# The last product of a retention and two-layer MoE kernel as seven half products

## The chip, the cores and the metric

The kernel runs on one core of one Trainium2 chip. The metric is the device time of one execution in microseconds, as the median of several runs. The profile shows one execution: TensorE (PE; its weight loads are PEld), VectorE (DVE), ScalarE (ACT), GpSimd (POOL), the DMA queues issued from SP, ACT and POOL, and the TensorE clock that was granted.

## The reference

```python
# q, k, v: (8, 8, 576, 64)
gamma = 1 - 2.0 ** (-5 - arange(8))                 # one per head
Dmat  = where(i >= j, gamma ** (i - j), 0)
x     = ((q @ k.T / 8) * Dmat) @ v                  # -> 4608 tokens x 512
a, b  = x @ w1, x @ w2                              # 512 x 1024 each
x2    = ((a * b) @ w3) @ w_out                      # 1024 x 1024, 1024 x 512
h     = x2 @ w_in2                                  # 512 x 2048
g     = h * clip(h + 3, 0, 6) / 6
out   = g @ w_out2                                  # 2048 x 512
```

The weights arrive as 64-bit floats. The kernel decodes each piece to 32 bits with two ScalarE and two VectorE operations (`weights`, L132).

## The kernel before, in words

Every large product is made from operands that are split in a high and a low part (a ScalarE cast writes the high part, a VectorE subtraction the low part): `mm3` (L123) issues three matmuls, high x high, high x low and low x high, into one bank of PSUM. Each matmul comes with its own weight load of 128x128.

The order of the work is written out by hand. `at(s, f)` (L113) puts a function into slot `s`; each `mm3`, and each matmul of the prologue, first calls `tick()` (L116), which runs the functions of the present slot. A slot fixes where an instruction stands in its engine's program, not when it runs: engines run their programs in order, and waits on data are added by the framework.

Four stages follow each other:

1. **Prologue** (L450 to L476). 32 matmuls of 256 columns on zeros warm TensorE up, and then `w3 @ w_out` is computed into `Wh`, `Wl` (eight tiles `Wps`, four banks, so the fifth tile waits until the first is read out by `w_hi` and `w_lo`). Beside it the first pieces of w1 and w2 are loaded and decoded (`order12`, L414), and the first attention tiles run as "excursions" (`ex`, L433): scores of tile t+1, then the products of tile t; a mask on VectorE (`p_mask`) follows the scores one slot later.
2. **moe1** (`ffn1`, L493): nine blocks of 512 tokens, 96 `mm3` each, with the excursions between them. It ends each half block with x2's operand sums for the next stage, stored to DRAM (`xod`), through the staging tiles `stg` and `stg_hi`. The blocks also hold jobs that prepare weights and store them to DRAM: `job_set` (L604) makes the seven sums of a pair of w_in2 pieces (`wid`), `job_q` (L626) decodes one of sixteen pieces of w_out2 (`wqd`). `E0` is the start of the last block.
3. **moe2's first product** (`run_set`, L733): six blocks of 768 tokens, eight sets each, already as seven half products per set (Strassen's scheme, Winograd's form), with 384 columns per matmul. `gate` (L705) makes g from each result and GpSimd's queue stores it to DRAM (`gd`).
4. **moe2's last product** (L829 to L864): nine blocks of 512 tokens. For each of 16 pieces of the 2048 inner columns g is loaded (`load_g`, two pieces per DMA), split (`g_hi`, `g_lo`) into one of two buffers, and used as the stationary operand for four groups of 128 tokens: `mm3` with 512 columns of w_out2 (all loaded before, `load_wq`). After 16 pieces ScalarE copies four banks out with the factor 1/6, and SP's queue stores them (`store`, L834).

```python
for t in range(BLK2 // 128):
    ...
    ts = slice(t * 128, t * 128 + 128)
    mm3(acc[t], gh[:, ts], gl[:, ts], w[:, m % 4, 0], w[:, m % 4, 1], m == 0, m == M2 - 1)
```

## Time and profile before

| | |
|---|---|
| median of 3 runs | 1514.9 us (1514.26 to 1515.38) |
| the profiled execution's own time | 1514.79 us |
| its span, first to last instruction | 1513.0 us |
| TensorE busy | 1497.9 us (99%) |
| VectorE, ScalarE, GpSimd busy | 775.7, 534.7, 254.5 us |
| granted TensorE clock, mean | 0.999 |
| moe2's last product, first to last matmul start | 1116.4 to 1508.9 us |

The page gives shares over the whole span; a stage has to be read from windows or from its own tiles. Busy time is the time in which at least one instruction of the engine runs; matmuls are pipelined and their records overlap, so the spacing of starts, not a record's length, says how fast they go. The profiled execution's time is 1.8 us longer than its span.

### The profile page before, as it was taken

To read this page: it belongs to the slowest core of one execution; us is meant where nothing else is said; L and a number is where in the kernel's file an instruction comes from. 1 tells how busy PE (TensorE), PEld (TensorE's weight loads), DVE (VectorE), ACT (ScalarE), POOL (GpSimd) and SP (SyncE) were. 2 spreads that over 40 slices of the span, in tenths; PEclk is the share of its full clock that TensorE was granted. 3 is DMA by queue.
4 is the path that set the end of the run, shared out by engine and by line. 5 is a ranking of instruction groups with operands and counts; after the bars stand their busy time and mean duration, and the time that the engine had idled before them with its cause. 6 is when DMAs were issued, how large, how long until landed. Compare 5 with 4: busy or idle time off the path is not lost. (4 is left out here: it accounts for less than half of the span.)

```text
span 1513.0 us, 23506 instructions
## 1 busy us (share of the span) xinstructions
PE 1497.9 (99%) x9248; PEld 1273.2 (84%) x9248; DVE 775.7 (51%) x1449; ACT 534.7 (35%) x883; POOL 254.5 (17%) x460
## 2 busy tenths in 40 slices
PE   8899999999999999999999999999999999999999
PEld 4478888888888888888899999999988888888887
DVE  6886565565655565653256666666652222222222
ACT  6473333333333342332233333333332222222222
POOL 3313212222222212200012323223310000000000
PEclk9999999999999999999999999999999999999999
DMA  9853647465656654524689464464872223333320
GB/s 326 255 181 98 215 147 217 152 209 162 202 167 182 202 167 161 182 91 145 256 324 344 170 260 171 190 251 154 329 262 104 91 91 133 139 139 140 139 84 28
DMA packets 121295, 274.58 MB, mean 181 GB/s; under 512 B 12784, under 2 KB 55792, under 8 KB 120160
## 3 DMA queue, kind: packets, MB, share of 16 engines
q1 hardware_dynamic: 48288, 144.72, 27.2%
q0 software_dynamic: 25856, 75.93, 15.6%
q10 hardware_dynamic: 47040, 52.43, 10.1%
q8 instruction: 72, 1.18, 0.3%
q14 instruction: 39, 0.32, 0.1%
HBM read 169.75 MB, written 103.28 MB: 180 GB/s over the span
## 5 line engine op out<-in xcount | busy, mean ns | idle before, releaser
L130 DVE TENSOR_TENSOR ghl<-gr,ghl 128x512 fp32r<-128x512 f32 x144 | 99.7, 693 | 287.7 <-ACT ghl L805 285.6
L125 PE MATMUL pb<-xop,wset 128*128 128x384 f32 x672 | 225.8, 336 | 2.6 <-DVE stghi L700 1.5
L127 PE MATMUL pb<-xop,wset 128*128 128x384 f32 x672 | 225.8, 336 | 0.0
L126 PE MATMUL pb<-xop,wset 128*128 128x384 f32 x672 | 225.5, 336 | 0.0
L127 PE MATMUL po<-wq,ghl 128*128 128x512 f32 x576 | 224.3, 389 | 0.0
L125 PE MATMUL po<-wq,ghl 128*128 128x512 f32 x576 | 224.2, 389 | 0.0
L126 PE MATMUL po<-wq,ghl 128*128 128x512 f32 x576 | 224.1, 389 | 0.0
L805 ACT CAST ghl<-gr 128x512 fp32r<-128x512 f32 x144 | 89.5, 622 | 275.8 <-PE po L127 275.7
L719 POOL DMA_DIRECT2D gd<-g x192 | 104.4, 544 | 361.4 <-DVE g L714 222.1
L186 POOL DMA_DIRECT2D qk<-in_qk_dram x144 | 84.6, 594 | 433.3 <-PE z L233 362.7
L710 ACT ACTIVATE stghi<-g,three 128x384 f32<-128x384 f32 x141 | 87.1, 617 | 128.8 <-DVE g L700 128.6
L125 PEld LDWEIGHTS pb<-xop,wset 128*128 128x128 f32 x672 | 126.2, 188 | 4.1 <-DVE stghi L700 1.9
L127 PEld LDWEIGHTS po<-wq,ghl 128*128 128x128 f32 x576 | 108.1, 188 | 23.4 <-DVE ghl L130 0.9
L125 PEld LDWEIGHTS po<-wq,ghl 128*128 128x128 f32 x576 | 108.1, 188 | 22.8 <-ACT ghl L805 0.5
L126 PEld LDWEIGHTS po<-wq,ghl 128*128 128x128 f32 x576 | 108.1, 188 | 22.4
L126 PEld LDWEIGHTS pb<-xop,wset 128*128 128x128 f32 x672 | 126.2, 188 | 0.0
L127 PEld LDWEIGHTS pb<-xop,wset 128*128 128x128 f32 x672 | 126.2, 188 | 0.0
L125 PE MATMUL pa<-xh,w1h 128*128 128x512 f32 x288 | 114.1, 396 | 0.0
L125 PE MATMUL px<-abh,Wh 128*128 128x512 f32 x288 | 114.0, 396 | 0.0
L125 PE MATMUL pb<-xh,w2h 128*128 128x512 f32 x288 | 112.3, 390 | 0.0
L126 PE MATMUL pa<-xl,w1h 128*128 128x512 f32 x288 | 112.2, 390 | 0.0
L127 PE MATMUL px<-abh,Wl 128*128 128x512 f32 x288 | 112.2, 390 | 0.0
(133 smaller groups left out, 2401.6 us busy)
## 6 DMA issues: line engine op xcount, KB each, us to landing
gd<-g POOLq DMA_DIRECT2D x192, 192.0 KB, 4.1
gr<-gd SPq DMA_DIRECT2D x72, 512.0 KB, 7.4
xop<-xod SPq DMA_DIRECT2D x42, 768.0 KB, 7.7
qk<-in_qk_dram POOLq DMA_DIRECT2D x144, 128.0 KB, 4.2
wset<-wid SPq DMA_DIRECT2D x8, 1792.0 KB, 12.9
wr<-in_w_dram SPq DMA_DIRECT2D x24, 512.0 KB, 11.8
kv<-in_kv_dram POOLq DMA_DIRECT2D x36, 256.0 KB, 4.6
kv<-in_kv_dram POOLq DMA_DIRECT2D x72, 128.0 KB, 4.2
```

The source lines that it names most:

```text
L125: nc.tensor.matmul(out=out_ap, lhsT=sh, rhs=mh, start=first, stop=False, **kw)
L126: nc.tensor.matmul(out=out_ap, lhsT=sh, rhs=ml, start=False, stop=False, **kw)
L127: nc.tensor.matmul(out=out_ap, lhsT=sl, rhs=mh, start=False, stop=last, **kw)
L130: eng.tensor_tensor(out=out_ap, in0=x, in1=y, op=ALU.subtract)
L186: nc.gpsimd.dma_start(out=x[rows, g].rearrange("d x a i -> d x (a i)"), in_=qk[2 * t + g].rearrange("d x (b a) i -> d x b (a i)", a=2)[:, ...
L710: nc.scalar.activation(out=c["r"], in_=src(), func=ACTF.Relu, bias=three)
L719: nc.gpsimd.dma_start(out=gd[:, m, p0:p0 + BLK], in_=c["g"])
L805: nc.scalar.copy(out=h, in_=x)
```

## The change

- The last product is made per 256 tokens as seven half products (`out_block`): 128 tokens x 1024 inner columns x 256 output columns each, that is 8 x 3 matmuls of 256 columns. Operands on g's side are four sums or differences of the raw quarters (`s_sum`, 128x1024), split by `prep` into one of three operand buffers two products ahead. Results are combined by two ScalarE copies and five VectorE additions of 128x256 per block; then SP stores 128x512 twice.
- g is loaded as quarters (`load_raw`: 128 tokens x 8 pieces, four per block, seven buffers). The gate now makes h x clip((h + 3)/6, 0, 1), so the factor 1/6 falls away at the end.
- The operand sums of w_out2 are made in moe1: `job` takes the place of `job_set` and `job_q`, eight of each kind, each with two decoded pieces, four sums, one cast and one subtraction of 128x1792 and two stores. The jobs of set n stand in block n+1, up to the last block. Seven products' weights are loaded late in moe2's first product, four as whole tiles (`q_tile`), three in twelve quarter units (`q_late`).
- w1's first pieces are decoded later (first at slot LEAD+48 instead of LEAD+41, four instead of five before moe1), and the first excursions move: -1 from LEAD+28 to LEAD+32, 0 from LEAD+35 to LEAD+38.
- A buffer for the signs of the last block's decoding is taken from another tile (`late_sign`), and two loads of x operands move (49 to 4, 54 to 52).

```diff
-    wqd = dram_p.tile([M2, 128, 2, DM], F32, name="wqd")
+    wqd = dram_p.tile([7, 128, NSET, 2, 256], F32, name="wqd")
...
-        order12 = [(LEAD + 41 + 6 * f, w1, f) for f in range(5)]
-        order12 += [(B0 - 3 + 11 * f // 2, x, n) for f, (x, n) in enumerate((
-            (w2, 0), (w2, 1), (w2, 2), (w2, 3), (w2, 4), (w1, 5), (w2, 5), (w1, 6), (w2, 6), (w1, 7), (w2, 7)))]
+        order12 = [(LEAD + 48 + 5 * f, w1, f) for f in range(4)]
+        order12 += [(B0 - 3 + 5 * f, x, n) for f, (x, n) in enumerate((
+            (w2, 0), (w2, 1), (w2, 2), (w1, 4), (w2, 3), (w2, 4), (w1, 5), (w2, 5), (w1, 6), (w2, 6), (w1, 7), (w2, 7)))]
...
-                    lambda tiles_=tiles_, fs=fs: (tiles_[0][:, :, fs], tiles_[1][:, :, fs]), (0, 4, 8, 9))
+                    lambda tiles_=tiles_, fs=fs: (tiles_[0][:, :, fs], tiles_[1][:, :, fs]), (0, 4, 7, 8))
...
-        ex = {-1: LEAD + 28, 0: LEAD + 35, 1: LEAD + 43, 2: LEAD + 52, 3: LEAD + 60, 4: B0 + 52, 5: B0 + 63, 6: B0 + 74, 7: B0 + 85}
+        ex = {-1: LEAD + 32, 0: LEAD + 38, 1: LEAD + 45, 2: LEAD + 52, 3: LEAD + 59, 4: B0 + 52, 5: B0 + 63, 6: B0 + 74, 7: B0 + 85}
...
-        def job_set(n, s):
-            weights(("i", n), s - 12, s, wf_p, stg[:, 512:1024], w_in2[n], None)
-            weights(("i", n + NSET), s - 8, s + 4, wf_p, stg[:, 0:512], w_in2[n + NSET], None)
+        def job(key, srcs, sums_of, outs, s):
+            weights((key, 0), s - 12, s, wf_p, stg[:, 512:1024], srcs[1], None)
+            weights((key, 1), s - 8, s + 4, wf_p, stg[:, 0:512], srcs[0], None)
 
             def sums():
-                nc.vector.tensor_tensor(out=as_[:, 4], in0=as_[:, 0], in1=as_[:, 1], op=ALU.add)
-                for o, a, b in ((5, 4, 2), (6, 2, 0), (7, 3, 5)):
-                    sub(nc.vector, as_[:, o], as_[:, a], as_[:, b])
+                for o, a, b, op in sums_of:
+                    nc.vector.tensor_tensor(out=as_[:, o], in0=as_[:, a], in1=as_[:, b], op=op)
 
             def hi():
                 nc.scalar.copy(out=stg_hi.bitcast(F32R), in_=stg[:, 256:2048])
@@ -617,28 +616,19 @@
                 sub(nc.vector, stg[:, 256:2048].bitcast(F32R), stg[:, 256:2048], stg_hi.bitcast(F32R))
 
             def store():
-                nc.scalar.dma_start(out=wid[n, :, 0], in_=stg_hi)
-                nc.scalar.dma_start(out=wid[n, :, 1], in_=stg[:, 256:2048])
+                for hl, t in enumerate((stg_hi, stg[:, 256:2048])):
+                    o = outs(hl)
+                    nc.scalar.dma_start(out=o, in_=t if len(o.shape) == 2 else t.rearrange("p (o n) -> p o n", o=7))
...
-            job_set(n, B0 + SPB * max(n, 1) + (12 if n else 44))
-        for m in range(M2):
-            b, i = divmod(m, 3) if m < 12 else (4 + (m - 12) // 2, m % 2)
-            job_q(m, B0 + SPB * (b + 2) + 40 + 8 * i, i)
+            job(("i", n), (w_in2[n + NSET], w_in2[n]), A_SUMS, lambda hl, n=n: wid[n, :, hl], B0 + SPB * n + SPB + 12)
+            job(("q", n), (w_out2[n], w_out2[n + NSET]), B_SUMS,
+                lambda hl, n=n: wqd[:, :, n, hl].rearrange("o p n -> p o n"), B0 + SPB * n + SPB + 44)
...
+        def late_sign():
+            signs[:] = [xo_p.tile([128, 4 * BLK1], I32, tag="xl", name="raw")[:, 1024:1536]]
+            nc.gpsimd.memset(signs[0], 0)
+
+        at(E0, late_sign)
         at(E0 + 14, open_late)
-        for i, s in enumerate((20, 26, 32, 38, 44, 49, 54)):
+        for i, s in enumerate((20, 26, 32, 38, 44, 4, 52)):
...
-                nc.scalar.activation(out=c["r"], in_=src(), func=ACTF.Relu, bias=three)
+                nc.scalar.activation(out=c["r"], in_=src(), func=ACTF.Relu, bias=half, scale=1.0 / 6.0)
 
             def f1():
                 c["g"] = src() if keep else g_tile()
                 nc.vector.scalar_tensor_tensor(
-                    out=c["g"], in0=c["r"], scalar=6.0, in1=src(), op0=ALU.min, op1=ALU.mult)
+                    out=c["g"], in0=c["r"], scalar=1.0, in1=src(), op0=ALU.min, op1=ALU.mult)
...
+        NB3 = NT // 256
+        POS = (0, 4, 3, 2, 5, 1, 6)
+        tq, un, ops = {}, {}, {}
+
+        def q_unit(p, u, dst):
+            tq[p, u] = dst
+            nc.sync.dma_start(out=dst.bitcast(F32), in_=wqd[POS[p], :, 2 * u:2 * u + 2].rearrange("p k h n -> p (k h n)"))
+
+        def q_tile(p):
+            w = wab_p.tile([128, 4, 1024], F32R, tag=WTAGS[p], name="wq")
+            for u in range(4):
+                tq[p, u] = w[:, u]
+            nc.sync.dma_start(out=w.bitcast(F32), in_=wqd[POS[p]].rearrange("p (u k) h n -> p u (k h n)", u=4))
+
+        def q_late(i):
+            w = ap["xl"].tile([128, 3, 1024], F32R, tag=f"s{4 + i}", name="wq")
+            for v in range(3):
+                q_unit(4 + (3 * i + v) // 4, (3 * i + v) % 4, w[:, v])
+
+        RAW = (9, 10, 0, 3, 4, 7, 8)
+        PARTS = ((1, 0), (1, 1), (0, 0), (0, 1))
+
+        def f32_unit(k):
+            if k not in un:
+                un[k] = ring(k, [128, 1024], F32, "unit")
+            return un[k]
+
+        def raw(b, h, kh):
+            return f32_unit(RAW[(4 * b + PARTS.index((h, kh))) % 7])
+
+        def load_raw(b, h, kh):
+            if b < NB3:
+                p0 = 256 * b + 128 * h
+                nc.sync.dma_start(out=raw(b, h, kh).rearrange("p (m t) -> p m t", t=128), in_=gd[:, 8 * kh:8 * kh + 8, p0:p0 + 128])
+
+        def op_tiles(q):
+            i = q % 3
+            if i not in ops:
+                if i == 0:
+                    ops[i] = [wf_p.tile([128, 1024], F32R, tag="wr", name="op") for _ in range(2)]
+                else:
+                    x = xo_p.tile([128, 2, 1024], F32R, tag=("xh", "xl")[i - 1], name="op")
+                    ops[i] = [x[:, 0], x[:, 1]]
+            return ops[i]
+
+        def s_sum(b, i):
+            if b < NB3:
+                o, x, y, f = (
+                    (1, (1, 0), (1, 1), ALU.add), (2, 1, (0, 0), ALU.subtract),
+                    (1, (0, 0), (1, 0), ALU.subtract), (1, (0, 1), 2, ALU.subtract))[i - 1]
+                t = [f32_unit(v) if isinstance(v, int) else raw(b, *v) for v in (x, y)]
+                nc.vector.tensor_tensor(out=f32_unit(o), in0=t[0], in1=t[1], op=f)
+
+        SRC = ((0, 0), 2, 1, (0, 1), 1, 1, (1, 1))
+
+        def prep(b, p, s):
+            b, p = b + p // 7, p % 7
+            if b == NB3:
+                return
+            c = {}
+
+            def src():
+                return f32_unit(SRC[p]) if isinstance(SRC[p], int) else raw(b, *SRC[p])
+
+            def hi():
+                nc.scalar.copy(out=op_tiles(7 * b + p)[0], in_=src())
+
+            def lo():
+                h, l = op_tiles(7 * b + p)
+                sub(nc.vector, l, src(), h)
+
+            if p in (4, 5):
+                at(s, lambda: s_sum(b, p - 1))
+            at(s + 1, hi)
+            at(s + 3, lo)
...
+                if (sb, k) == (NSB - 1, 7):
+                    s = now[0]
+                    at(s + 5, lambda: s_sum(0, 2))
+                    prep(0, 1, s + 9)
+                    at(s + 9, lambda: load_raw(0, 0, 1))
...
-                        load_wq(k - 1)
-                    if k == 6:
-                        tail()
-        G = NB2 * M2
-        g_hi(0)
-        g_lo(0)
+                        q_tile(k - 1)
+                    if k == 2:
+                        for part in PARTS[:3]:
+                            load_raw(0, *part)
+                    if k == 4:
+                        s_sum(0, 1)
+                    if k == 5:
+                        prep(0, 0, now[0])
+                    if k > 4:
+                        q_late(k - 5)
         pending.pop()()
-
-        def store(jb, t, po):
-            c_ = {}
-
-            def f0():
-                c_["o"] = stg[:, 512 * t:512 * t + 512]
-                nc.scalar.activation(out=c_["o"], in_=po, func=ACTF.Copy, scale=1.0 / 6.0)
-
-            def f1():
-                half, c = divmod((jb * BLK2 + t * 128) % (2 * BLK), BLK)
-                c += (jb * BLK2 + t * 128) // (2 * BLK) * BLK
-                r0 = c // HB1 * BLK1 + half * HB1 + c % HB1
-                nc.sync.dma_start(out=out[r0:r0 + 128, :], in_=c_["o"])
-
-            at(now[0], f0)
-            at(now[0] + 1, f1)
-
-        for i in range(G):
-            jb, m = divmod(i, M2)
-            if i % 2 == 0 and i // 2 + XE < G // 2:
-                at(now[0], lambda i=i: load_g(i // 2 + XE))
-            if i + 1 < G:
-                at(now[0], lambda i=i: g_hi(i + 1))
-                at(now[0] + 1, lambda i=i: g_lo(i + 1))
-            gh, gl = g_t[i]
-            w = wq[m // 4]
-            for t in range(BLK2 // 128):
-                if m == 0:
-                    acc[t] = ps.tile([128, DM], F32, tag="b", name="po")
-                ts = slice(t * 128, t * 128 + 128)
-                mm3(acc[t], gh[:, ts], gl[:, ts], w[:, m % 4, 0], w[:, m % 4, 1], m == 0, m == M2 - 1)
-                if m == M2 - 1:
-                    store(jb, t, acc[t])
+        q_late(3)
...
+        def out_block(b):
+            c = {}
+            z = b % 2
+            o = [stg[:, 1024 * z + 512 * h:1024 * z + 512 * h + 512] for h in range(2)]
+            u, U, V = (stg_hi[:, 512 * i + 256 * z:512 * i + 256 * z + 256] for i in range(3))
+            p0 = 256 * b
+
+            def bank(k):
+                c[k] = ps.tile([128, 512], F32, tag="b", name="po")[:, 0:256]
+
+            def store(h):
+                hh, g = divmod((p0 + 128 * h) % (2 * BLK), BLK)
+                g += (p0 + 128 * h) // (2 * BLK) * BLK
+                r0 = g // HB1 * BLK1 + hh * HB1 + g % HB1
+                nc.sync.dma_start(out=out[r0:r0 + 128, :], in_=o[h])
+
+            def add2(out_ap, a, k):
+                return lambda: add(out_ap, a, c[k])
+
+            for p, (k, first) in enumerate((
+                    ("A", True), ("B", True), ("D", True), ("A", False), ("C", True), ("D", False), ("C", False))):
+                if first:
+                    bank(k)
+                if p == 0:
+                    for part in PARTS[:3]:
+                        at(now[0], lambda part=part: load_raw(b + 1, *part))
+                if p == 3:
+                    at(now[0] + 4, lambda: load_raw(b + 1, 0, 1))
+                prep(b, p + 2, now[0])
+                if p in (4, 5):
+                    at(now[0] + 5, lambda p=p: s_sum(b + 1, p - 3))
+                h, l = op_tiles(7 * b + p)
+                for kt in range(8):
+                    ts = slice(128 * kt, 128 * kt + 128)
+                    w = tq[p, kt // 2][:, 512 * (kt % 2):512 * (kt % 2) + 512]
+                    mm3(c[k], h[:, ts], l[:, ts], w[:, 0:256], w[:, 256:512], first and kt == 0, kt == 7, skip_group_check=True)
+                if p == 0:
+                    at(now[0], lambda: nc.scalar.copy(out=u, in_=c["A"]))
+                elif p == 3:
+                    at(now[0], lambda: nc.scalar.copy(out=o[0][:, 256:512], in_=c["A"]))
+                else:
+                    at(now[0], add2(*{1: (U, u, "B"), 2: (V, U, "D"), 4: (o[1][:, 0:256], V, "C"),
+                                      5: (o[0][:, 0:256], U, "D"), 6: (o[1][:, 256:512], U, "C")}[p]))
+                if p > 4:
+                    at(now[0] + 1, lambda p=p: store(p - 5))
+
+        for b in range(NB3):
+            out_block(b)
```

## Rows read from the trace of the kernel before

**Rows 1.** The page, part 1: busy time, share of the span and instructions per engine.
```profile
PE 1497.9 (99%) x9248; PEld 1273.2 (84%) x9248; DVE 775.7 (51%) x1449; ACT 534.7 (35%) x883; POOL 254.5 (17%) x460
```

**Rows 2.** Waits of TensorE over the span, longest first: us in total, times, longest us.
```profile
PE Wps L464 <- DVE Wl L130: 4.5, 1, 4.5
...
```

**Rows 3.** The tile `po`: duration ns min/median/max, first and last start us, form.
```profile
L125 PEld LDWEIGHTS po<-wq,ghl x576: 186/188/189, 1116.4 to 1508.2; 128*128 128x128 f32 x192
L125 PE MATMUL po<-wq,ghl x576: 389/389/500, 1116.4 to 1508.4; 128*128 128x512 f32 x192
...
L127 PE MATMUL po<-wq,ghl x576: 388/389/502, 1117.1 to 1508.9; 128*128 128x512 f32 x192
```

**Rows 4.** Timeline of TensorE, 1400 to 1412 us (start us, us): first and last of 55 matmuls.
```profile
1399.62 0.39 PE L125 MATMUL po<-wq,ghl 128*128 128x512 f32 x1
...
1411.86 0.39 PE L125 MATMUL po<-wq,ghl 128*128 128x512 f32 x1
```

**Rows 5.** Windows, moe1 and last stage: us, busy (x) per engine, PEclk, DMA share, GB/s.
```profile
410.00:475.00 65.00, 65.00 (x490) 53.63 (x489) 37.51 (x73) 22.93 (x36) 11.96 (x21) 1.00 0.57 177
...
1300.00:1400.00 100.00, 100.00 (x443) 82.81 (x442) 25.62 (x37) 27.45 (x45) 0.00 (x0) 1.00 0.36 127
```

**Rows 6.** Timeline of TensorE, 900 to 912 us: two starts of 384 columns, 69 matmuls apart.
```profile
899.99 0.33 PE L125 MATMUL pb<-xop,wset 128*128 128x384 f32 x1
...
911.96 0.34 PE L125 MATMUL pb<-xop,wset 128*128 128x384 f32 x1
```

**Rows 7.** The warm-up: timelines from 5.5 and 5.3 us (merged), the tile, 6 to 6.5 us.
```profile
5.24 1.95 PE L454 MATMUL zero<-Wh 128*128 128x256 f32 x15
...
5.07 2.23 PE L454 MATMUL zero<-Wh 128*128 128x256 f32 x17
...
L454 PE MATMUL zero<-Wh x6: 280/283/283, 5.8 to 6.4; 128*128 128x256 f32 x6
```

**Rows 8.** Groups of instructions by line and form: busy us, mean ns | idle before.
```profile
L130 DVE TENSOR_TENSOR stg<-stg,stghi 128x512 fp32r<-128x512 f32 x33 | 22.8, 691 | 2.6
...
L130 DVE TENSOR_TENSOR stg<-stg,stghi 128x1024 fp32r<-128x1024 f32 x17 | 20.8, 1226 | 0.0
...
L581 ACT CAST stghi<-stg 128x1024 fp32r<-128x1024 f32 x17 | 17.9, 1056 | 3.5 <-DVE stg L130 3.5
...
L130 DVE TENSOR_TENSOR stg<-stg,stghi 128x1792 fp32r<-128x1792 f32 x8 | 16.2, 2025 | 8.2 <-ACT stghi L614 8.2
...
L614 ACT CAST stghi<-stg 128x1792 fp32r<-128x1792 f32 x8 | 13.6, 1698 | 29.5 <-DVE stg L130 29.5
...
L264 DVE TENSOR_TENSOR S<-S,z 128x256 f32<-128x256 f32 x24 | 9.9, 411 | 0.0
```

**Rows 9.** The tile `po` again: the copies at the end of a block.
```profile
L839 ACT ACTIVATE stg<-po x36: 597/598/601, 1159.1 to 1509.3; 128x512 f32<-128x512 f32 x36
```

**Rows 10.** Timeline, 1160 to 1185 us: a cast and the subtraction that waits for it.
```profile
1161.63 0.61 ACT L805 CAST ghl<-gr 128x512 fp32r<-128x512 f32 x1
...
1162.28 0.69 DVE L130 TENSOR_TENSOR ghl<-gr,ghl 128x512 fp32r<-128x512 f32 x1 [2.51 <-ACT ghl L805]
```

**Rows 11.** DMA issues: count, KB each, median us from issue to landing.
```profile
gr<-gd SPq DMA_DIRECT2D x72, 512.0 KB, 7.4
...
xod<-stg ACTq DMA_DIRECT2D x12, 448.0 KB, 4.5
```

**Rows 12.** Timeline of VectorE in the prologue, 30 to 90 us.
```profile
41.23 1.28 DVE L218 TENSOR_TENSOR P<-sc,mask 128x512 f32<-128x512 f32 x2
42.43 1.28 DVE L130 TENSOR_TENSOR Wl<-Wps,Wh 128x512 fp32r<-128x512 f32 x2
```

**Rows 13.** Windows in the prologue, columns as in rows 5.
```profile
45.00:45.50 0.50, 0.50 (x2) 0.34 (x1) 0.50 (x2) 0.00 (x0) 0.00 (x0) 0.50 1.15 311
46.00:46.50 0.50, 0.50 (x3) 0.26 (x2) 0.47 (x2) 0.00 (x0) 0.00 (x0) 0.88 0.97 262
76.00:84.00 8.00, 8.00 (x94) 4.48 (x92) 7.93 (x17) 6.14 (x12) 3.97 (x7) 1.00 0.65 197
```

More of the change, by code (lines that the diff above doesn't have):

```diff
@@ L81, in retention_moe_kernel @@
     wid = dram_p.tile([NSET, 128, 2, 7 * 256], F32, name="wid")
-    wqd = dram_p.tile([M2, 128, 2, DM], F32, name="wqd")
+    wqd = dram_p.tile([7, 128, NSET, 2, 256], F32, name="wqd")
     gd = dram_p.tile([128, M2, NT], F32, name="gd")
-    three = const_p.tile([128, 1], F32, name="three")
+    half = const_p.tile([128, 1], F32, name="half")
     stg = const_p.tile([128, 2048], F32, name="stg")
@@ L302, in retention_moe_kernel @@
     with tc.manual_schedule():
-        nc.vector.memset(three, 3.0)
+        nc.vector.memset(half, 0.5)
         ph1 = ExitStack()
@@ L619, in store @@
             def store():
[L620 to L621 removed]
+                for hl, t in enumerate((stg_hi, stg[:, 256:2048])):
+                    o = outs(hl)
+                    nc.scalar.dma_start(out=o, in_=t if len(o.shape) == 2 else t.rearrange("p (o n) -> p o n", o=7))
             for d, f in ((10, sums), (11, hi), (14, lo), (19, store)):
                 at(s + d, f)
[L626 to L635 removed]
+        A_SUMS = ((4, 0, 1, ALU.add), (5, 4, 2, ALU.subtract), (6, 2, 0, ALU.subtract), (7, 3, 5, ALU.subtract))
+        B_SUMS = ((4, 0, 1, ALU.subtract), (5, 2, 4, ALU.subtract), (6, 2, 0, ALU.subtract), (7, 3, 5, ALU.subtract))
         for n in range(NSET):
[L638 to L641 removed]
+            job(("i", n), (w_in2[n + NSET], w_in2[n]), A_SUMS, lambda hl, n=n: wid[n, :, hl], B0 + SPB * n + SPB + 12)
+            job(("q", n), (w_out2[n], w_out2[n + NSET]), B_SUMS,
+                lambda hl, n=n: wqd[:, :, n, hl].rearrange("o p n -> p o n"), B0 + SPB * n + SPB + 44)
         wset, xop = {}, {}
@@ L703, in g_tile, with gate @@
             return g_p.tile([128, BLK], F32, tag="g", name="g")
-        def gate(src, sb, m, half, keep=True):
+        def gate(src, sb, m, h, keep=True):
             c = {}
@@ L714, in f1 @@
                 nc.vector.scalar_tensor_tensor(
-                    out=c["g"], in0=c["r"], scalar=6.0, in1=src(), op0=ALU.min, op1=ALU.mult)
+                    out=c["g"], in0=c["r"], scalar=1.0, in1=src(), op0=ALU.min, op1=ALU.mult)
             def f2():
-                p0 = (2 * sb + half) * BLK
+                p0 = (2 * sb + h) * BLK
                 nc.gpsimd.dma_start(out=gd[:, m, p0:p0 + BLK], in_=c["g"])
@@ L783, in run_set @@
             pending.append(end)
-        wq = {}
-        XE = 4
-        def load_wq(i):
-            wq[i] = w = wab_p.tile([128, 4, 2, DM], F32R, tag=WTAGS[i], name="wq")
-            for m in range(4):
-                nc.sync.dma_start(out=w[:, m].bitcast(F32), in_=wqd[4 * i + m])
-        gr, g_t, acc = {}, {}, {}
-        def load_g(q):
-            jb, i = divmod(q, M2 // 2)
-            gr[q] = x = ring(7 * NSB + q, [128, 2, BLK2], F32, "gr")
-            nc.sync.dma_start(out=x, in_=gd[:, 2 * i:2 * i + 2, jb * BLK2:jb * BLK2 + BLK2])
@@ L801, in g_hi @@
-        def g_hi(i):
-            x = gr[i // 2][:, i % 2]
-            hl = wf_p.tile([128, 2, BLK2], F32R, tag="wr", name="ghl")
-            g_t[i] = h, l = hl[:, 0], hl[:, 1]
-            nc.scalar.copy(out=h, in_=x)
-        def g_lo(i):
-            sub(nc.vector, g_t[i][1], gr[i // 2][:, i % 2], g_t[i][0])
-        def tail():
-            for q in range(XE):
-                load_g(q)
+        NB3 = NT // 256
[4 more added lines that the diff above has]
+            nc.sync.dma_start(out=dst.bitcast(F32), in_=wqd[POS[p], :, 2 * u:2 * u + 2].rearrange("p k h n -> p (k h n)"))
```

8 lines of the change are left out of this document (removed).

## The prediction

> **What bounds the kernel now.** I read the page first: TensorE is busy 1497.9 of 1513.0 us, while VectorE stands at 51% and ScalarE at 35% [rows 1]. Then the waits of TensorE: the longest is 4.5 us, in the prologue [rows 2]. So the time is the number of matmuls times their spacing, plus a few stalls. Third, the stage that is replaced: the product `po` takes 3 x 576 = 1728 matmuls, the first starting at 1116.4 us and the last at 1508.9 us [rows 3]: 392.5 us, or 26% of the span. Inside it the spacing is even: 55 matmuls from 1399.62 to 1411.86 us, 12.24/54 = 226.7 ns each [rows 4]. 1727 x 226.7 ns is 391.5 us, so the old stage carries only 1.0 us beside its matmuls. VectorE and ScalarE are busy a quarter of it, and the granted clock is full [rows 5]. The stage is bound by the spacing alone, and a record's own length (389 ns) is not that spacing: neighbours overlap.
>
> **The new product: columns saved, matmuls added.** Before: 9 blocks x 16 pieces x 4 x 3 = 1728 matmuls of 512 columns. After: 18 blocks x 7 half products x 8 pieces x 3 = 3024 of 256 columns. Columns fall to 7/8 (884,736 to 774,144), but there are 1296 more matmuls, so what each costs beside its columns decides. The spacing at 384 columns is (911.96 - 899.99)/69 = 173.5 ns [rows 6]. Against 226.7 ns at 512 that is 53.2 ns for 128 columns, and the same step down gives 120.3 ns at 256. That is an extrapolation, so I looked for a row with 256 columns: the 32 warm-up matmuls, each with its own weight load. In their later part 15 lie in 1.95 us with records of 283 ns, (1.95 - 0.28)/14 = 119 ns; 17 lie in 2.23 us, (2.23 - 0.28)/16 = 122 ns [rows 7]. I take 120 ns, where the extrapolation and the warm-up meet, and keep 119 and 122 ns. Sum: 3023 x 120 ns = 362.8 us instead of 392.5 us, **-29.7 us** (-32.8 at 119 ns, -23.7 at 122 ns). Of the 1/8 of columns (49 us at full value) some 17 us go back into 1296 x 13 ns of cost per matmul.
>
> A row that speaks against this is the weight load: its record lasts 188 ns in every stage [rows 3], longer than 120 ns. If loads could not overlap each other or the running matmul, the load would be the spacing. The rows deny it: 384-column matmuls, each with its load, follow each other every 173.5 ns [rows 6], and the warm-up's every 120 ns [rows 7]. The Trainium skill (TensorE: Matmul & The Clock Gate, Part 3, The mechanism) says that a weight load overlaps a running matmul only where the row group differs, and all matmuls here use the whole array. By that rule load and columns would add up, the same page giving 107 ns for a load of 128 columns and 107 ns for 256 columns at the full clock, an estimate of 214 ns and some 647 us for the stage; by the rows it is 363 us. The trace does not agree with the rule.
>
> **What must hide beside the matmuls.** One half product is 24 x 120 ns = 2.88 us, a block 20.2 us. ScalarE has seven casts of 128x1024 at 1.06 us [rows 8] and two copies from PSUM of 256 columns, each under the 0.60 us of a 512-wide one [rows 9]: 8.6 us at most. VectorE has seven subtractions and four operand sums of 128x1024 at 1.23 us and five additions from PSUM of 128x256 at 0.41 us [rows 8]: 15.6 us of 20.2 us. Both fit on average, but VectorE goes from a quarter busy to three quarters, so order matters. Operands lie in three buffers, so `prep` for product p+2 can write only when product p-1 is through: it has two products, 5.8 us. The tight run is across products 2 to 4: addition, sum, cast, subtraction for product 4, then addition, sum, cast, subtraction for product 5, each waiting for the one before: 2 x (0.41 + 1.23 + 1.06 + 1.23) = 7.9 us. Handing over costs about 0.04 us (a cast from 1161.63 for 0.61 us, the subtraction at 1162.28 [rows 10]), four times, and the last matmul's tail some 0.25 us at the start: 8.3 us. It has from the end of product 1 to the start of product 5, 3 x 2.88 = 8.6 us. I cost it at nothing, with only 0.3 us of cover per block; if that is gone, product 5 is what is late.
>
> The loads: four of 512 KB per block (2 MB in 20.2 us, 104 GB/s) against one per 5.4 us before; with the stores that is near the 127 GB/s of the old stage [rows 5], but the runs shrink from 2 KB to 512 B. Stores of 448 KB in 512 B runs land in 4.5 us, and 512 KB in 2 KB runs in 7.4 us [rows 11], so short runs are no visible burden. Three loads are issued at the start of a block and first needed 4 products and 5 steps later, some 13 us on. The sync queue holds four loads and two stores per block, and a load's buffer has been free since the block before. Cost nothing; if they come late, VectorE's next operand sum waits, and the additions queued behind it hold the banks. The weights for products 4 to 6 are twelve new loads, the last three issued as the stage starts and needed 17 us later; nothing.
>
> **moe1.** Sixteen small jobs become eight larger ones. VectorE: per job four sums at 0.41 us and one 1792-wide subtraction of 2.03 us against two of 512 at 0.69 us, 8 x 2.3 = 18 us more over 650 us; ScalarE eight casts of 1.70 us, less what sixteen smaller ones took [rows 8]. In a block of moe1 VectorE is busy some 38 of 65 us and TensorE all of it [rows 5]. The last block, which had no job, now takes a pair, some 13 us of VectorE; attention is over by then. The job's stores come before x2's first writing of the staging tile by some 16 steps of 0.68 us. Nothing. The gate's scale and bias change no operation.
>
> **The prologue.** The 4.5 us stall waits for the first `Wl`; VectorE has the P mask ahead of it, from 41.23 us, and starts `Wl` at 42.43 us [rows 12]; TensorE goes on when the first `Wl` is done, near 43.1 us. The change puts the first excursion four steps later, so the mask falls behind all four `Wl`: `Wl` starts 1.2 us earlier. After the stall the granted clock is 0.50 (the 1.2 GHz level), and back at full within the half microsecond after 46 us [rows 13]; TensorE had done nothing for 4.5 us before. Three us at half speed lose 1.5 us. If the shorter stall escapes that, the gain is 2.7 us. The moved matmuls of the scores stay before the stall's end either way. What could eat it is VectorE, busy 7.9 of 8 us just before moe1 [rows 13]; but two pieces' decoding (two 512-wide operations of 0.69 us each [rows 8]) moves behind the last `xl` that moe1 waits for, so it can follow. By my count of VectorE's program (four `Wl`, one decoded piece, then the mask) the mask then ends some 5 us after the first `Wl` starts, and the excursion that needs it stands six products behind the stall. I take **-2.0 us**, with 0 and -2.7 as ends; the no-gain end is that this region is paced by VectorE and loads.
>
> **The end.** After the last matmul (start 1508.9) came a 0.60 us copy, then a store to 1513.0. Now an addition of 0.41 us, and a shorter matmul: **-0.3 us** [rows 3, 8, 9].
>
> **Sum.** -29.7 - 2.0 - 0.3 = -32.0 us. The profiled execution took 1514.8 us (span 1513.0), 0.1 us below the median of the runs shown. 1514.8 - 32.0 = 1482.8 us.
>
> **The rivals.**
> - *The prologue gives nothing* (the stall is filled by something else, so this part does not do what it says): 1484.8 us, chance 0.15. For it: VectorE's full slices. Against: the mask stands ahead of `Wl` in plain sight.
> - *VectorE's chain binds.* If each of its eight links costs 0.15 us more than I count, 8.3 us becomes 9.5 us and product 5 waits 0.9 us per block, 16 us in 18 blocks: 1499 us, chance 0.12. For: 0.3 us of cover. Against: neighbouring VectorE instructions overlap by some 0.08 us (the mask pair's 1.28 us is followed after 1.20 us) [rows 12], which I did not count.
> - *The raw loads come late.* If 512 B runs took three times as long, the third load of a block lands 3 us after its use, about 1 us of it past VectorE's slack: 18 us, 1501 us, chance 0.05.
> - *The weight load sets the spacing*: slower. At 188 ns per load the stage takes 3024 x 0.188 = 568.5 us, +176 us, some 1689 us. It decides from 392.5/3023 = 130 ns: above that spacing the change loses by itself. For: the load's 188 ns, and that the warm-up always loads the same weights, over 2 us only. Against: [rows 6, 7]. Chance 0.04. The skill's rule above points this way too.
>
> **How the numbers follow.** My forecast has 0.60; 0.04 stay for what I do not see. Its own bounds: 119 ns and the full prologue gain give 1479.0; 122 ns and neither prologue nor end gain give 1491.1. The range starts at 1478 and reaches to 1493, to take in a chain that loses half a microsecond in some blocks; it leaves out the strong forms of the later rivals. A measurement of this kernel tells about 0.2%, 3 us, from no change. All cases but the last rival lie over 3 us below: faster 0.95, same 0.01, slower 0.04.
>
> **What would show it.** The matmuls of the last stage at 120 ns start to start, 24 per 2.88 us, a stage of some 363 us from first to last start, TensorE without waits in it, VectorE near 77% and ScalarE near 41%. Waits of TensorE for VectorE or ScalarE once per block would show the chain; waits of VectorE for loads, the second; a spacing near the weight load's record, the last. In the prologue: the stall near 3 us, the clock perhaps full after it. I am wrong if the spacing is over 122 ns or the stage has waits above 9 us in all.

## The result, and the profile after

The changed kernel takes **1486.6 us** (median of 4 runs, 1485.66 to 1487.72) against 1515.1 us for the kernel before on the same chip (4 runs, 1514.26 to 1515.38): a ratio of 0.981, with a 95% interval of 0.980 to 0.983. The forecast was 1482.8 us, faster, with 1478 to 1493 as its range. The time came out 3.8 us above the forecast: the replaced stage gave what was forecast to a tenth of a microsecond, and something beside it was lost.

The page of the kernel after, part 1, shows it still bound by TensorE; VectorE went from 51% to 64% [rows 1]:

```profile
PE 1469.7 (99%) x10544; PEld 1313.3 (88%) x10544; DVE 956.4 (64%) x1617; ACT 568.8 (38%) x857; POOL 254.2 (17%) x461
```

The product's tile `po` in the kernel after (number, then duration in ns min/median/max, first and last start in us, form), to be read against [rows 3]:

```profile
L125 PEld LDWEIGHTS po<-wq,op x1008: 187/192/192, 1118.0 to 1480.6; 128*128 128x128 f32 x168
L125 PE MATMUL po<-wq,op x1008: 280/283/284, 1118.2 to 1480.7; 128*128 128x256 f32 x168
...
L127 PE MATMUL po<-wq,op x1008: 279/283/283, 1118.4 to 1480.9; 128*128 128x256 f32 x168
```

From the first start to the last are 362.7 us, and 362.7/3023 = **120.0 ns** from one matmul to the next. No matmul of the stage starts more than 0.121 us after the one before it, so there is no wait in it. Neither the record's 283 ns nor the weight load's 192 ns is the spacing. A window of 100 us inside the stage (us, busy and count for PE, PEld, DVE, ACT and POOL, granted clock, DMA share, GB/s) shows VectorE at 73% and ScalarE at 38%, where the stage before had 26% and 27% [rows 5]:

```profile
1240.00:1340.00 100.00, 100.00 (x836) 100.00 (x835) 72.63 (x81) 38.22 (x45) 0.00 (x0) 1.00 0.46 130
```

TensorE's waits (us in total, times, longest us) are where the rest has to be looked for. These are those of the kernel after; in the kernel before the first was 4.5 us [rows 2]:

```profile
PE Wps L464 <- DVE Wl L130: 3.2, 1, 3.2
PE pb L125 <- DVE stghi L695: 2.4, 2, 1.6
...
PE pb L125 <- ACT stg L736: 1.7, 2, 1.1
PE pb L125 <- DVE g L695: 0.8, 1, 0.8
...
PE pa L126 <- DVE xl L130: 0.6, 1, 0.6
```

In moe2's first product (`pb`) the kernel before had, beside a wait of 0.7 us that both kernels have, only these:

```profile
PE pb L125 <- DVE stghi L700: 1.5, 1, 1.5
PE pb L125 <- DVE stg L700: 0.3, 1, 0.3
```

**The balance.** The span goes from 1513.0 to 1484.7 us, -28.3 us. By the starts of the first and last matmul of each stage in the two traces (moe1 is counted from the first matmul of its second product, also called `pb`; this lies some 4 us behind moe1's very first matmul, and behind the wait for `xl`):

| stretch | before | after | difference | forecast |
|---|---|---|---|---|
| start to moe1's first `pb` matmul | 86.6 | 84.5 | -2.1 | -2.0 |
| from there to moe2 | 676.5 | 676.3 | -0.2 | 0 |
| moe2's first product | 353.4 | 357.4 | **+4.0** | 0 |
| last product, first to last start | 392.4 | 362.7 | -29.7 | -29.7 |
| last start to the end | 4.1 | 3.8 | -0.3 | -0.3 |

So the question for the experiments is the line of +4.0 us in a stage whose matmuls the change does not touch, and whether the other lines are right for the reasons given. Setting each of that stage's 2016 matmuls beside the same one of the kernel before shows where it is lost: 0.8 us in the first set, 2.4 us between 1098 and 1111 us, and 0.9 us at the end; some 0.3 us is won back near 800 us.

### The profile page after: what moved, and what is told of

It is laid out like the page before. It is cut to its first block, busy times and chain, and to the rows that moved or that the text cites. A ratio compares the mean times of both kernels' runs of the same rounds, so it can differ in the third digit from the quotient of the medians.

```text
span 1484.7 us, 26113 instructions
## 1 busy us (share of the span) xinstructions
PE 1469.7 (99%) x10544; PEld 1313.3 (88%) x10544; DVE 956.4 (64%) x1617; ACT 568.8 (38%) x857; POOL 254.2 (17%) x461
## 5 line engine op out<-in xcount | busy, mean ns | idle before, releaser
L125 PE MATMUL po<-wq,op 128*128 128x256 f32 x1008 | 285.3, 283 | 0.0
L126 PE MATMUL po<-wq,op 128*128 128x256 f32 x1008 | 285.3, 283 | 0.0
L127 PE MATMUL po<-wq,op 128*128 128x256 f32 x1008 | 285.3, 283 | 0.0
L130 DVE TENSOR_TENSOR op<-unit,op 128x1024 fp32r<-128x1024 f32 x126 | 154.1, 1224 | 92.8 <-ACT op L845 92.8
L845 ACT CAST op<-unit 128x1024 fp32r<-128x1024 f32 x126 | 132.2, 1049 | 186.1 <-DVE unit L831 164.6
L127 PEld LDWEIGHTS po<-wq,op 128*128 128x128 f32 x1008 | 193.5, 192 | 0.0
L126 PEld LDWEIGHTS po<-wq,op 128*128 128x128 f32 x1008 | 193.5, 192 | 0.0
L125 PEld LDWEIGHTS po<-wq,op 128*128 128x128 f32 x1008 | 193.5, 192 | 0.0
L705 ACT ACTIVATE stghi<-g,half 128x384 f32<-128x384 f32 x141 | 87.1, 617 | 132.7 <-DVE g L695 132.7
L127 PE MATMUL pa<-xh,w1l 128*128 128x512 f32 x288 | 112.2, 390 | 0.0
```

The source lines that it names most:

```text
L125: nc.tensor.matmul(out=out_ap, lhsT=sh, rhs=mh, start=first, stop=False, **kw)
L126: nc.tensor.matmul(out=out_ap, lhsT=sh, rhs=ml, start=False, stop=False, **kw)
L127: nc.tensor.matmul(out=out_ap, lhsT=sl, rhs=mh, start=False, stop=last, **kw)
L130: eng.tensor_tensor(out=out_ap, in0=x, in1=y, op=ALU.subtract)
L705: nc.scalar.activation(out=c["r"], in_=src(), func=ACTF.Relu, bias=half, scale=1.0 / 6.0)
L845: nc.scalar.copy(out=op_tiles(7 * b + p)[0], in_=src())
```

## The experiments

Each kernel was timed beside the kernel before on the same chip. The kernel before had medians of 1514.9 to 1515.3 us there, so times of different kernels can be set against each other to within half a microsecond.

**The prologue alone, and all but the prologue.** The first kernel puts the prologue's new order into the kernel before; the second is the kernel after with the old order.

```diff
-        order12 = [(LEAD + 41 + 6 * f, w1, f) for f in range(5)]
...
+        order12 = [(LEAD + 48 + 5 * f, w1, f) for f in range(4)]
...
-        ex = {-1: LEAD + 28, 0: LEAD + 35, 1: LEAD + 43, 2: LEAD + 52, 3: LEAD + 60, 4: B0 + 52, ...
+        ex = {-1: LEAD + 32, 0: LEAD + 38, 1: LEAD + 45, 2: LEAD + 52, 3: LEAD + 59, 4: B0 + 52, ...
```

> The kernel before with the change's prologue alone (w1's first pieces later, the first excursions moved). Theory A (the mask falls behind Wl and the shift is kept to moe1): the stall before the fifth tile falls from 4.5 to some 3.2 us, moe1's first pb matmul starts near 84.5 us instead of 86.6 us, and the time is 2.1 us below the kernel before. Theory B (of those 2.1 us some 0.9 us were only loads that happened to land earlier in that one profile): 1.2 us below. Rival (the prologue gives nothing, VectorE paces it): within 0.3 us of the kernel before.

> The changed kernel with the prologue of before put back: all of the rest of the change. Theory A: 2.1 us above the changed kernel (some 1488.7 us against 1486.6). Theory B: 1.2 us above. Rival: no difference. The last stage stays at 362.7 us from first to last start in all cases, and what is lost at the end of moe2's first product stays.

The prologue alone: 1513.8 us (11 runs, 1511.7 to 1515.8), a ratio of 0.999 (0.998 to 1.000), so -1.5 us by medians, with an interval that reaches no change. Everything but the prologue: 1489.0 us (4 runs, 1488.1 to 1490.4), 2.4 us above the kernel after. The first `Wps` matmul starts anywhere between 8.4 and 9.1 us, so the stretch from it to moe1's first `pb` matmul measures this edit better. It is 77.45 and 77.30 us in the two kernels with the old order, and 76.02 and 76.37 us in the two with the new one: **1.2 us**. In the second kernel moe2's first product took 358.7 us, 1.3 us more than in the kernel after, which makes up the rest of its 2.4 us. This stage's waits differ between executions, and nothing in the edit explains that part.

In the timelines of the kernel after, the mask now stands behind all four `Wl`, as forecast (the order was the other way round in [rows 12]):

```profile
39.50 2.48 DVE L130 TENSOR_TENSOR Wl<-Wps,Wh 128x512 fp32r<-128x512 f32 x4
...
43.22 1.28 DVE L218 TENSOR_TENSOR P<-sc,mask 128x512 f32<-128x512 f32 x2
```

The stall shrank by the mask pair's 1.2 to 1.3 us, from 4.5 to 3.2 us. But the granted clock still fell to 0.50, the 1.2 GHz level, as it had before [rows 13]. Windows of the kernel after, columns as above:

```profile
41.00:42.00 1.00, 1.00 (x3) 0.48 (x2) 1.00 (x3) 0.79 (x2) 0.00 (x0) 0.84 1.01 295
42.00:43.00 1.00, 1.00 (x2) 0.34 (x1) 0.96 (x2) 0.00 (x0) 0.00 (x0) 0.50 1.02 352
...
45.00:46.00 1.00, 1.00 (x4) 0.52 (x3) 0.97 (x3) 0.00 (x0) 1.00 (x2) 0.96 0.99 295
```

The time at half speed is as long as before, so its 1.5 us were not won.

**The +4 us: loads brought forward.** The timeline of the kernel after, just before the last product starts, shows VectorE waiting for a store of g and TensorE waiting behind it:

```profile
1101.88 0.56 DVE L695 TENSOR_TENSOR g<-stg,pb 128x384 f32<-128x384 f32 x1 [2.34 <-DMA gd<-g]
...
1104.51 0.45 PE L125 MATMUL pb<-xop,wset 128*128 128x384 f32 x1 [1.14 <-ACT stg L736]
...
1107.62 0.44 PE L125 MATMUL pb<-xop,wset 128*128 128x384 f32 x1 [0.75 <-DVE stghi L695]
```

The gate's result needs a `g` tile, and the tile is free when its store has landed. Ahead of this stretch and in it, SP's queue also fetches weights and the first three raw quarters. The third kernel issues these three loads two sets earlier:

```diff
-                    if k == 2:
+                    if k == 0:
                         for part in PARTS[:3]:
```

> The changed kernel with the first three loads of g's quarters issued two sets earlier, before the weight tiles, when the DMA engines are a third busy. Theory (the 2.7 us of new TensorE waits at the end of moe2's first product come from loads that crowd out the stores of g, so that VectorE waits for a g tile): the 2.3 us wait of VectorE for such a store goes or shrinks, TensorE's waits after 1090 us fall from 2.7 to about 0.8 us, and the time falls by 1 to 2 us. Rival (the extra VectorE and ScalarE work for the first operands, not the DMA, makes TensorE wait): the waits and the time stay within 0.5 us.

It took 1485.7 us (5 runs, 1484.1 to 1486.8), 1.0 us less than the kernel after by medians; the intervals of the two ratios overlap (0.979 to 0.982 here), so the trace has to carry it. Its span is 1.6 us shorter, and moe2's first product takes 355.6 us, 1.8 us less: the 2.4 us between 1098 and 1111 us are gone, and the start of the stage lost some 0.6 us more in this execution. VectorE's wait for g's stores, in the waits of the kernel after and then of this one (1040 to 1125 us):

```profile
DVE g L695 <- DMA gd<-g: 2.3, 1, 2.3
```

```profile
DVE g L695 <- DMA gd<-g: 0.5, 1, 0.5
```

The stores themselves land sooner. DMA issues from 1090 to 1100 us (KB each, median us from issue to landing) in the kernel before, after, and in this one:

```profile
gd<-g POOLq DMA_DIRECT2D x5, 192.0 KB, 6.1
```

```profile
gd<-g POOLq DMA_DIRECT2D x5, 192.0 KB, 8.4
```

```profile
gd<-g POOLq DMA_DIRECT2D x5, 192.0 KB, 6.6
```

In the kernel after the DMA engines are busy all through these 10 us (share 1.01, 424 GB/s; 0.97 and 360 GB/s before, 0.95 and 332 GB/s in this kernel). So 2.4 of the +4 us is g's stores, slowed down by the raw loads for the new stage. VectorE waits for the tile, and TensorE for VectorE and ScalarE. The expectation's rival, the new stage's first cast and subtraction, does not hold: both still stand in this stretch of the third kernel, and TensorE does not wait there.

**The +4 us: the join.** After the third kernel one wait is left before the last product, with this order on VectorE (timeline of the third kernel):

```profile
1113.69 1.23 DVE L130 TENSOR_TENSOR op<-unit,op 128x1024 fp32r<-128x1024 f32 x1 [1.05 <-ACT op L845]
...
1114.84 0.55 DVE L695 TENSOR_TENSOR g<-stg,pb 128x384 f32<-128x384 f32 x1
1115.44 0.44 PE L125 MATMUL pb<-xop,wset 128*128 128x384 f32 x1 [0.77 <-DVE g L695]
```

The new stage's operand subtraction (1.23 us) stands ahead of the gate's last read of a bank which TensorE needs to go on. The next kernel keeps the early loads and prepares that operand one step later:

```diff
-                    prep(0, 1, s + 9)
+                    prep(0, 1, s + 10)
```

> The early raw loads of the run before, and in the last set the cast and subtraction for product 1 one step later, so that the addition that frees bank C stands ahead of the 1.23 us subtraction on VectorE. Theory (the 0.8 us wait at the join, 1.0 us with its restart, is this subtraction in front of that addition): the wait after 1110 us goes, and the time is 1.0 us below the run with early loads alone and some 2 us below the changed kernel. Rival (the bank would be late anyway): no difference from the early loads alone.

It took 1484.5 us (5 runs, 1483.7 to 1487.2), 1.1 us less than the third kernel by medians, which the scatter of the runs does not resolve. The wait is gone from the trace, moe2's first product takes 354.9 us, 0.7 us less than in the third kernel, and the span is 1.3 us shorter.

Of the +4.0 us that leaves some 0.8 us at the start of that stage. The DMA issues around 760 us show one store of moe1's last block in the kernel after, and in the kernel before:

```profile
xod<-stg SPq DMA_DIRECT2D x1, 896.0 KB, 10.8
```

```profile
xod<-stg SPq DMA_DIRECT2D x1, 896.0 KB, 5.8
```

ScalarE's first copy of the stage needs the tile that this store reads. The store takes 5.5 us in the first kernel, which has the new prologue alone, and 9.9 us in the second, which has all but it. So it comes from the rest of the change. Ten profiles have that rest: the store takes 9.9 to 11.3 us in them and the stage's first set loses 0 to 1.3 us, in the same order, so the loss is what the store takes beyond some 10 us. The last block now has a job with its loads and stores, and two loads of x operands that were moved; which of them it is was not tried.

**VectorE's chain.** Two kernels add work of a known size to VectorE in each block of the last product: one addition of 0.41 us, done twice after product 2, or one operand sum of 1.22 us, done twice before product 5.

```diff
+                if p == 2:
+                    at(now[0], add2(V, U, "D"))
```

> The changed kernel with one addition of 128x256 done twice (V, after product 2), 0.33 us more on VectorE's chain in every block. Theory (the chain from product 1's end to product 5 ends some 0.6 us before it is needed): nothing changes, the stage stays at 362.7 us and the time within 1 us of the changed kernel. Rival (the chain has no cover left): 18 blocks x 0.3 us = 6 us more.

```diff
                 at(s, lambda: s_sum(b, p - 1))
+                if p == 5:
+                    at(s, lambda: s_sum(b, p - 1))
```

> The changed kernel with the operand sum before product 5 done twice: 1.13 to 1.22 us more on VectorE's chain in every block, which ends some 0.6 us before product 5 needs it. Theory (cover of about 0.6 us, then one for one): TensorE waits for VectorE once per block by some 0.6 us, 18 x 0.6 = 11 us, with a slow restart each time perhaps 14 us; the stage grows from 362.7 to 373 to 377 us. Rival (the cover is larger than the chain shows, because two products of operands are ahead): no wait, 362.7 us.

The small addition changes nothing: 1486.4 us (one run), and the stage takes 362.7 us as before. It stands inside VectorE's chain, where the sum behind it now starts 0.78 us after it instead of 0.33 us (compare the chain of the kernel after below):

```profile
1127.85 0.87 DVE L695 TENSOR_TENSOR stghi<-stghi,po 128x256 f32<-128x256 f32 x2
1128.63 1.22 DVE L831 TENSOR_TENSOR unit<-unit 128x1024 f32<-128x1024 f32 x1
```

So the chain has at least 0.45 us of cover. With the second sum the kernel takes 1497.7 us (one run), and the tile `po` grows to 375.0 us:

```profile
L125 PE MATMUL po<-wq,op x1008: 277/283/357, 1117.0 to 1491.8; 128*128 128x256 f32 x168
...
L127 PE MATMUL po<-wq,op x1008: 277/283/387, 1117.3 to 1492.0; 128*128 128x256 f32 x168
```

Its waits have a new line, once per block:

```profile
PE po L127 <- DVE op L130: 5.9, 18, 0.3
```

The stage loses 12.3 us, 0.68 us in each of 18 blocks (in most of them one matmul starts 0.61 us after the one before instead of 0.12, and three more start some 0.05 to 0.1 us late; the waits show 5.9 us of the 12.3). The added sum makes the chain 1.26 us longer (the two sums take 2.48 us together), so the chain had **about 0.6 us of cover**. This is the chain as it runs in the kernel after:

```profile
1124.15 0.42 DVE L695 TENSOR_TENSOR stghi<-stghi,po 128x256 f32<-128x256 f32 x1 [0.30 <-PE po L127]
1124.49 1.22 DVE L831 TENSOR_TENSOR unit<-unit 128x1024 f32<-128x1024 f32 x1
1126.88 1.23 DVE L130 TENSOR_TENSOR op<-unit,op 128x1024 fp32r<-128x1024 f32 x1 [1.17 <-ACT op L845]
1128.02 0.41 DVE L695 TENSOR_TENSOR stghi<-stghi,po 128x256 f32<-128x256 f32 x1
1128.35 1.22 DVE L831 TENSOR_TENSOR unit<-unit 128x1024 f32<-128x1024 f32 x1
1130.76 2.45 DVE L130 TENSOR_TENSOR op<-unit,op 128x1024 fp32r<-128x1024 f32 x2 [1.19 <-ACT op L845]
```

The addition, the sum, the cast (seen as VectorE's wait of 1.17 us) and the subtraction follow one another twice, and VectorE has no other gap.

**The stall in the prologue.** In the kernel after VectorE waits 1.6 us for the raw piece that it decodes from 33.29 us, and does `make_rates`, 3.6 us of small operations, behind that piece (from 34.64 us) and ahead of `Wl`. This kernel puts `make_rates` one slot earlier, so that it can fall into the wait:

```diff
-        at(LEAD + 25, make_rates)
-        at(LEAD + 24, lambda: (load_qk(1), load_kv(1)))
+        at(LEAD + 24, lambda: (load_qk(1), load_kv(1), make_rates()))
```

> The changed kernel with the 3.5 us of rate tables moved one slot up on VectorE, into its 1.6 us of idle time ahead of the decoding of the ninth w3 piece. Theory (the stall before the fifth tile is VectorE's program order, and the clock falls only after the long stall): Wl starts 1.5 us earlier, the stall falls from 3.2 to 1.7 us, the granted clock stays at 1.00 between 40 and 46 us, which gives 1.5 us more; moe1 starts 2 to 3 us earlier unless VectorE's last xl holds it. Rival (VectorE's total work up to moe1 paces it): the wait at pa for xl grows from 0.6 us by what the stall loses, and the time stays within 0.5 us.

1484.3 us (4 runs, 1483.4 to 1485.3), 2.3 us less. `make_rates` now starts at 31.48 us and the 1.6 us are gone; the stall is 1.5 us and the clock does not fall; moe1's first `pb` matmul starts 2.5 us earlier, at 82.0 us. Its wait, and the window from 36 to 48 us:

```profile
PE Wps L463 <- DVE Wl L130: 1.5, 1, 1.5
```

```profile
36.00:48.00 12.00, 10.51 (x113) 5.98 (x113) 10.31 (x21) 6.37 (x12) 4.08 (x7) 1.00 1.04 323
```

**All three together.** Early loads, the join, and `make_rates`:

> The three edits together: early raw loads, the join, the rate tables. If they add up: 2 us from the end of moe2's first product and 1.5 to 3 us from the prologue, 1481.5 to 1483 us. If VectorE paces the prologue: 1484.5 us.

1483.6 us (4 runs, 1482.0 to 1484.1; ratio 0.979, 0.978 to 0.981): the fastest version, 3.0 us below the kernel after, but not below `make_rates` alone by more than the runs scatter. moe2's first product is 354.7 us and the stall 1.7 us. In its profile a later wait had grown, for VectorE's `xl` just before moe1, from 0.6 us in the kernel after to

```profile
PE pa L126 <- DVE xl L130: 1.3, 1, 1.3
```

and moe1's first `pb` matmul starts at 84.1 us, nearly as late as in the kernel after. Two other waits stand on the way, of 0.5 us for a load of q and k at 54 us and of 0.75 us for `kv` at 65 us. The prologue's program is that of the kernel with `make_rates` alone, where that matmul came 2.2 us sooner: what the shorter stall gives is taken back by later waits in one execution and not in another.

**Weights later.** If it is the weights' loads that delay g's stores, issuing the late ones one set later should do as much as the early raw loads:

```diff
-                    if k > 4:
-                        q_late(k - 5)
+                    if k > 5:
+                        q_late(k - 6)
...
+        q_late(2)
         q_late(3)
```

> The changed kernel with the twelve late quarter units of weights each one set later (the last six as the last product starts); the loads of g's quarters stay where the change has them. Theory (any large load in the 1085 to 1105 us stretch crowds out the stores of g, the weights as much as the 512 B runs): VectorE's 2.3 us wait for a store near 1100 us shrinks below 1 us, TensorE's waits there (1.1 and 0.8 us) go or move behind 1108 us, and moe2's first product shortens from 357 to 355 or 356 us. Rival (it is the 512 B runs of g's quarters): the waits near 1100 us stay as they are, 357 us. If the units come too late, TensorE waits for them in products 4 to 6 of the first block, near 1130 us.

> The three edits together (early raw loads, the join, the rate tables) and the weights' units one set later. Theory: no wait of VectorE for a store of g after 1085 us, moe2's first product at some 354 us, and a time of 1482.5 to 1483.5 us, at or a little below the three edits alone. Rival (the stores are already through with the early raw loads): no difference from the three edits.

Both expectations missed. Alone the edit gives 1490.2 us (4 runs, 1487.8 to 1491.0); on top of the best version 1486.3 us (5 runs, 1483.9 to 1488.8). The waits near 1103 and 1107 us stay, and the first batch was issued at 1093.9 us, as in the kernel after (1094.0 us): a slot fixes the order on SP's queue, and the batch goes when its tile is free. So this run does not tell whether those weights slow down the stores. What it shows is a new wait of TensorE in the last product, 2.1 us, with no releaser named:

```profile
PE po L125 <- issue: 2.1, 1, 2.1
```

VectorE's timeline names it. The operand sum at 1136.32 us waited for a raw quarter; the addition that frees the bank stands behind it and ends at 1137.87 us, and TensorE goes on at 1137.98 us. In the kernel after the same sum ran at 1133.12 us without a wait:

```profile
1136.32 1.23 DVE L831 TENSOR_TENSOR unit<-unit 128x1024 f32<-128x1024 f32 x1 [2.87 <-DMA unit<-gd]
1137.46 0.41 DVE L695 TENSOR_TENSOR stg<-stghi,po 128x256 f32<-128x256 f32 x1
```

SP's timeline says why the quarter was late. Nine weight loads were issued from 1112.78 us, where the kernel after had six, and the first three raw quarters of the next block, two of which the sum adds up, stand behind them:

```profile
1112.78 7.22 SPq L786 DMA_DIRECT2D wq<-wqd  x9
1120.21 12.11 SPq L813 DMA_DIRECT2D unit<-gd  x3
```

On top of the best version the same sum waits 4.0 us and TensorE 3.2 us, in the slowest of its five runs (1488.8 us); two others, 1483.9 and 1484.3 us, are about as fast as the best version, so the wait need not be there in each. This is the third rival's mechanism, made by hand. Behind the wait the matmuls are 0.21 us apart for some 3 us instead of 0.12, the granted clock being 0.50 from 1139 to 1142 us, and the stage takes 366.6 and 367.7 us, 4 to 5 us more.

The last kernel also tells something of the prologue. It has `make_rates` in the earlier slot, and yet its stall is 2.9 us and the clock falls, because here VectorE waits for ScalarE's `sign` of the next piece:

```profile
37.85 0.69 DVE L152 SCALAR_TENSOR_TENSOR w3f<-w3f,sign 128x512 int32<-128x512 int32 x1 [0.95 <-ACT sign L148]
```

```profile
36.00:48.00 12.00, 9.14 (x81) 4.47 (x82) 9.03 (x16) 7.09 (x12) 3.87 (x7) 0.86 1.04 309
```

So of three profiles with that edit two have the short stall.

## Why the prediction was right, step by step

- **Spacing, -29.7 us: right** (-29.7). The extrapolation from 512 and 384 columns, and 2 us of warm-up [rows 4, 6, 7], gave 120 ns; the stage ran 3024 matmuls at 120.0 ns. The steps are 53.2 and 53.5 ns for 128 columns each, so some 13 ns per matmul do not shrink with the columns. The rival of the weight load is dead: loads of 192 ns follow each other every 120 ns over 363 us. By the rule of the Trainium skill that I set against the rows (TensorE: Matmul & The Clock Gate, Part 3, The mechanism), the stage would have taken some 647 us, an estimate; this trace does not agree with it. That section also lets a load go ahead by a background weight buffer; no run here tells how the loads overlap. One side remark was off, and the sum does not use it: by these steps the eighth of the columns is worth 46 us, not 49.
- **The end, -0.3 us, and moe1, nothing: right** (-0.3 and -0.2 us).
- **"I cost it at nothing", VectorE's chain: right**, and tight as stated. I had 0.3 us of cover; it is about 0.6 us, and as neighbours overlap VectorE is busy 73% and not 77%. The mechanism of the rival is real: one operand sum more per block costs 12.3 us.
- **The raw loads inside the stage: right** as the change orders them. No start in the stage is late, the loads land in 5.7 us (median), and at 0.46 the DMA share is far from full. At the stage's start it is closer than I had it: the second block's second quarter lands at 1131.99 us, 1.1 us before the sum that reads it. The runs with three more weight loads ahead of them show what the rival described: quarter late, sum late, addition behind it late, and the bank with it.
- **The prologue, -2.0 us: right in size by luck.** The order changed as I read it, and the stall lost the mask's 1.2 us. The other part, half speed escaped, did not come in this profile; where it came with the same program (the kernel with a second sum), the stretch from the first `Wps` matmul to moe1's first `pb` one was 74.3 us, against 75.6 to 76.4 us in the six kernels with this prologue whose clock fell, so 1.5 us was a fair price. 1.2 us is what the edit is worth; the rest of the -2.1 us between the two profiles is an earlier first matmul, 8.5 instead of 9.1 us, which varies from run to run.
- **The step that failed** is "The weights for products 4 to 6 are twelve new loads, [...] needed 17 us later; nothing", with "Cost nothing" for the raw loads. I asked when these loads are needed, and not whom they hold up while they run. They share the DMA engines with g's stores, which VectorE waits for: 2.4 us, shown for the raw loads and not for the weights. Beside it the sum has no term for the seams at all. The first subtraction of the new stage, which stands ahead of the old stage's last gate on VectorE, costs 0.7 to 0.9 us, and a store that lands 5 us later at the first seam 0.8 us. With the 0.3 us won back near 800 us these make up the +4.0 us.

What stays open: whether it is the number of bytes or their 512-byte runs that slow g's stores, and whether the weights' loads take part; which part of the last block of moe1 slows the 896 KB store; and why ScalarE and the loads of the prologue are later in some executions, so that the three edits do not add up there.

## What to carry to other kernels

To price a change of tile size, take the spacing of starts from at least two sizes in the trace, extrapolate, and look for any matmul of the new size, even a warm-up: the fixed cost per matmul decides what a scheme with fewer columns and more matmuls gives. Then go to the seams: for each load that is moved or added, ask which store shares the DMA engines with it at that time and who waits for that store's tile; and for each first instruction of the new stage, which last instruction of the old one stands behind it on the same engine. Where a chain is hidden with little cover, a run that adds one operation of known length measures the cover.

## What was not expected of the hardware

After a stall of some 3 us in the prologue the granted clock fell in some executions and not in others. Two kernels with a stall of 3.0 us each have these windows from 36 to 48 us, the one with the join moved (0.86) and the one with a second sum in the chain (1.00):

```profile
36.00:48.00 12.00, 9.00 (x81) 4.46 (x82) 9.90 (x25) 5.77 (x10) 3.84 (x7) 0.86 1.04 315
```

```profile
36.00:48.00 12.00, 8.95 (x110) 5.26 (x110) 10.09 (x27) 5.89 (x11) 3.14 (x7) 1.00 1.04 317
```

The edits of both lie a thousand microseconds later, so the prologue's program is the same. The stalls of 1.5 and 1.7 us left the clock full; the 2.9 us of the last kernel and the wait of 2.1 us in the last product, with the weights moved, did not. In the kernel after, the fall shows in the slice from 41 to 42 us, when TensorE had been running again since 40.24 us. A forecast for a stall of this length can only give the clock's part a chance. Half speed also costs less than a doubling: in the last product the 256-column matmuls start 213 ns apart at 0.50 and 120.0 ns apart at 1.00, so what each costs beside its columns (some 13 ns at full speed) does not show at half.
